# Loading v on all 128 partitions, and keeping attention's packed values and last results in SBUF, in a fused attention and two-MLP kernel

## The chip, the cores and the metric

The kernel runs on one core of a Trainium2 chip. The time is device microseconds of one execution; lower is better. Three runs of the kernel before took 1675.51, 1675.57 and 1678.95 us, with a median of 1675.57 us. Five engines work at once and meet only at semaphores: TensorE (PE, with its weight loads shown as PEld), VectorE (DVE), ScalarE (ACT), GpSimd (POOL) and SyncE (SP), which issues nearly all DMA transfers.

## The reference

Three stages follow each other. First comes an attention that is done twice: 32 learned rows p per head attend to k and v of that head and give 32 packed values; then each row of q attends to these 32 values. There are 8 batches of 8 heads, 576 positions and 64 columns a head.

```python
scale = 1.0 / np.sqrt(q.shape[-1])
def sm_attn(qq, kk, vv):
    s = scale * np.matmul(qq, kk.transpose(0, 1, 3, 2))
    s = s - np.max(s, axis=-1, keepdims=True)
    a = np.exp(s)
    a = a / (np.sum(a, axis=-1, keepdims=True) + 1e-09)
    return np.matmul(a, vv)
p_packed = sm_attn(p, k, v)
out = sm_attn(q, p_packed, p_packed)
```

The result, as 4608 tokens of 512 columns, goes through two MLPs with 2048 hidden columns. The first has a rational function in its middle, the second h * cos(h).

```python
h = x @ w_in
h2 = h * h
h3 = h2 * h
P = a[0] + a[1] * h + a[2] * h2 + a[3] * h3
Q = 1.0 + np.abs(b[0]) * np.abs(h) + np.abs(b[1]) * h2
g = P / (Q + 1e-06)
x = g @ w_out                    # first MLP
h = x @ w_in2; g = h * np.cos(h) # second MLP
out = g @ w_out2
```

All four weight matrices come as 64-bit floats, 8 MB each, and are turned into 32-bit ones on the chip.

## The kernel before, in words

**Attention** works in 16 units u, each of one batch and four heads. For a unit, `load` (lines 435 to 452) brings p, k, q and v into SBUF, three buffers each. `trans` (L468) turns k and q on PE in nine 128x128 transposes each, and `copied` (L474) takes them from PSUM on ACT. `scores` (L497) multiplies p with k, in eight matmuls that use 64 rows and 32 columns of the array. `max1`, `exp1` (L515) and `recip1` are the softmax. `turn_exp` (L533, L535) turns the exponentials, four 128x128 transposes and two narrow matmuls, because the positions have to lie on the partitions for the next product. `pack` (L548) multiplies them with v in 20 matmuls: v lies in SBUF as [128 partitions, 4 heads, 5 pieces, 64], where the fifth piece fills only 64 partitions. `packed`, `turned` and `taken` scale and turn the packed values into the tile `lhpp`. `scores` once more multiplies q with them, and a second softmax (`turn2`, `max2`, `less_max2`, `exp2`, `sum2`, `recip2`, `scaled2`, `turn_back`) gives the tile `a2T`, which `keep_attn` (L606) writes to DRAM. `keep_pack` (L566) writes `lhpp` to the DRAM tensor `ppt`.

Where v is loaded, six transfers make a unit: four of 32 partitions with runs of 256 floats, and two of 32 partitions with runs of 64 floats (L446, L448).

**First MLP.** Its 128 items are 16 half batches c of eight pieces i. The packed values are folded into the first weights: `m_load` (L667) reads `ppt` back into the tile `pt`, and `m_prod` (L692) multiplies it with w_in1. Each batch needs four such products, which `m_hi` (ACT) and `m_lo` (DVE, L705) split into a high and a low part. An item is then a `front` (L737, 12 matmuls for each of two halves), some 14 steps on ACT, DVE and POOL for the rational function, and four `back` (L774) that multiply with w_out1. **Second MLP.** 144 items of the same form, with another function.

**Weights.** `convert` turns one 128-row piece of a weight: `w_load` brings it into one of two `raw` buffers, `w_exp` and `w_low` (ACT, L359 and L362), `w_abs` and `w_join` (DVE, L368 and L378) rebuild 32-bit floats; for w_out there are also `w_hi` (ACT) and `w_lo` (POOL). The first eight pieces of w_in1 and of w_out1 are turned while attention runs, the other eight of each after it. Of the 16 SBUF places of w_out1 (`wo0` to `wo15`), EARLY = 8 exist from the start. The others lie in memory that attention uses, and open when all of attention is done (`open_right`), together with the PSUM pool that `back` adds into.

**Order.** All instructions are listed as steps with a key. A planner (`Plan.order`) picks steps by key among those that could start, and writes the order of each engine; the table WANTED shifts the key of each kind of step. On the chip each engine runs its list strictly in that order, and SP's transfers are issued in list order too.

Of the kernel before, what the change touches and what calls it, by code (L numbers as in the profile page):

```python
# [9 lines left out]
F32 = mybir.dt.float32  # L10
# [17 lines left out]
class Plan:  # L28
# [14 lines left out]
        "a2_hi": 440, "a2_lo": 373, "a2_load": -22, "absolute": -628, "back 0": 104, "back 1": 169,  # L43
        "clipped": 70, "copied k": 251, "copied q": 43, "cosine": 245, "cubic 0": 228,
        "cubic 1": -452, "denom": -187, "done1": -328, "done2": -87, "doubled": 357, "exp1": 189,
        "exp2": 14, "exp_copied 0": -32, "exp_copied 1": 522, "front 0": -261, "front 1": -372,
        "keep_attn": 271, "keep_out": 425, "keep_pack": 48, "less_max2": -596, "lin 0": -168,
        "lin 1": -278, "load k": 275, "load p": -435, "load q": -220, "load v": 93, "lower 0": -109,
        "lower 1": 78, "m_hi": -93, "m_lo": 32, "m_load": -254, "m_prod": -307, "max1": -559,
        "max2": -95, "open_left": -187, "open_right": 541, "over 0": 72, "over 1": 202, "pack": 436,  # L50
        "packed": -313, "ratio": -102, "recip1": 165, "recip2": 77, "reduced 0": 285,
        "reduced 1": -222, "rounded": 209, "rsqrt": 308, "scaled2": 49, "scores 0": -225,
        "scores 1": 191, "slope": -116, "square": -380, "store": 355, "sum2": 21, "taken p": -208,
        "taken pp": 108, "times": -128, "trans k": 275, "trans q": 147, "turn2": 46,
        "turn_back": -404, "turn_exp": 79, "turned p": 64, "turned pp": 562, "upper 0": -141,
# [6 lines left out]
        "x_load": -33, "x_out": -508,  # L62
# [139 lines left out]
def pack_attention_moe_moe_kernel(  # L202
# [42 lines left out]
    EARLY = 8  # L245
# [24 lines left out]
    for pool, home, tags in (  # L270
# [5 lines left out]
        *((f"pt{g}", "cp", (f"pt{g}",)) for g in range(NG)),  # L276
# [8 lines left out]
        ("x0", "xp", ("x0",)),  # L285
# [10 lines left out]
        ("lhpp", "tp", ("lhpp0", "lhpp1")),  # L296
# [6 lines left out]
        ("a2T", "tp", tuple(f"a2T{i}" for i in range(9))),  # L303
# [15 lines left out]
    ppt = dram("ppt", NU, [P, P])  # L319
# [115 lines left out]
    def load(u, nm):  # L435
# [3 lines left out]
        if nm == "p":  # L439
            nc.sync.dma_start(t[:, 0, :], p[b, hs].rearrange("h n d -> (h n) d"))  # L440
        elif nm == "v":


            rows = v[b, hs].rearrange("h (p c) d -> p h c d", c=2 * NT9)
            for j in range(4):
                nc.sync.dma_start(t[32 * j : 32 * (j + 1), :, 0:4, :], rows[:, :, 4 * j : 4 * j + 4, :])  # L446
            for e in range(2):
                nc.sync.dma_start(t[32 * e : 32 * (e + 1), :, 4, :], rows[:, :, 16 + e, :])  # L448
        else:

            src = {"k": k, "q": q}[nm]
            nc.sync.dma_start(t, src[b, hs].rearrange("h (p c) d -> (h p) c d", c=2 * NT9))
# [655 lines left out]
```

## Time and profile before

| what | us |
|---|---|
| median of three runs | 1675.57 |
| the profiled execution | 1677.82 |
| its span | 1675.9 |
| PE busy in the span | 1581.6 (94%) |
| DVE busy | 1289.6 (77%) |
| ACT busy | 1021.1 (61%) |
| POOL busy | 308.3 (18%) |

The profile shows one execution. The span is what the engines' records cover; the execution is 1.9 us longer. A share over the whole span is a mean over attention, the first MLP and the second, which have different limits, so the rows further down split it by stretches of time. The granted clock of PE in a stretch is given as a share of its full 2.4 GHz, so that 0.50 is the lower level of 1.2 GHz. A 32-bit matmul appears in the trace as two passes, each with its weight load; a transpose as one pass.

### The profile page before, as it was taken

To read this page: it belongs to the slowest core of one execution; us is meant where nothing else is said; L and a number is where in the kernel's file an instruction comes from. 1 tells how busy PE (TensorE), PEld (TensorE's weight loads), DVE (VectorE), ACT (ScalarE), POOL (GpSimd) and SP (SyncE) were. 2 spreads that over 40 slices of the span, in tenths; PEclk is the share of its full clock that TensorE was granted. 3 is DMA by queue.
4 is the path that set the end of the run, shared out by engine and by line. 5 is a ranking of instruction groups with operands and counts; after the bars stand their busy time and mean duration, and the time that the engine had idled before them with its cause. 6 is when DMAs were issued, how large, how long until landed. Compare 5 with 4: busy or idle time off the path is not lost.

```text
span 1675.9 us, 26699 instructions
## 1 busy us (share of the span) xinstructions
PE 1581.6 (94%) x10176; PEld 1347.9 (80%) x10176; DVE 1289.6 (77%) x2025; ACT 1021.1 (61%) x1706; POOL 308.3 (18%) x246
## 2 busy tenths in 40 slices
PE   4776579999999999999999999999999999999998
PEld 3444278999999999999998888888888888888887
DVE  2655888999999999999998876666676757576664
ACT  3666788989899899898975543333333334333332
POOL 0223433333343343333321100000000000000000
PEclk7888689999999999999999999999999999999999
DMA  8998431211211121213242210101010101101010
GB/s 253 243 278 243 123 122 36 68 47 64 68 48 63 41 69 60 63 48 135 90 153 84 82 45 7 38 13 38 14 38 8 35 9 26 25 14 38 1 25 26
DMA packets 84383, 120.75 MB, mean 72 GB/s; under 512 B 19232, under 2 KB 61216, under 8 KB 84256
## 3 DMA queue, kind: packets, MB, share of 16 engines
q1 hardware_dynamic: 83872, 118.53, 24.1%
q8 instruction: 80, 1.31, 0.3%
q10 hardware_dynamic: 384, 0.52, 0.1%
q14 instruction: 47, 0.39, 0.1%
HBM read 85.99 MB, written 33.03 MB: 71 GB/s over the span
## 4 chain that ended last, share of the span: by engine, by line
PE 86%; DMA 4%; DVE 4%; ACT 3%; issue 1%; POOL 1%; SPq 1%; POOLq 0%; ACTq 0%
PE acc L774 46%; PE b L753 24%; PE b L737 11%; PE b L692 2%; DMA raw<-in_moe_w_in_dram 1%; PE b L468 1%; PE b L497 1%; DMA v_in<-in_v_dram 1%; DMA raw<-in_moe_w_out_dram 1%; ACT sc L362 0%; DVE T L868 0%; ACT sc L359 0%; DVE U L868 0%; ACT e L515 0%; DMA q_in<-in_q_dram 0%
## 5 line engine op out<-in xcount | busy, mean ns | idle before, releaser
L774 PE MATMUL acc<-gh,wo 128*128 128x288 f32 x2048 | 418.2, 298 | 9.0 <-ACT gh L900 9.0
L774 PE MATMUL acc<-wo,gh 128*128 128x512 f32 x1152 | 359.2, 393 | 0.0
L774 PEld LDWEIGHTS acc<-gh,wo 128*128 128x128 f32 x2048 | 332.0, 190 | 26.9 <-issue 15.9
L774 PE MATMUL acc<-gl,wo 128*128 128x288 f32 x1024 | 304.3, 297 | 1.0 <-DVE gl L903 0.9
L774 PEld LDWEIGHTS acc<-wo,gh 128*128 128x128 f32 x1152 | 216.3, 188 | 49.6
L857 POOL TENSOR_TENSOR U<-U,V 128x576 f32<-128x576 f32 x128 | 182.7, 1437 | 360.8 <-DVE T L872 116.3
L774 PE MATMUL acc<-wo,gl 128*128 128x512 f32 x576 | 226.7, 394 | 0.0
L891 ACT ACTIVATE U<-U 128x512 f32<-128x512 f32 x144 | 90.6, 630 | 203.2 <-DVE U L887 203.1
L903 DVE TENSOR_TENSOR gl<-V,gh 128x512 fp32r<-128x512 f32 x144 | 99.4, 690 | 136.8 <-PE acc L774 135.3
L836 ACT ACTIVATE T<-b 128x512 f32<-128x512 f32 x144 | 85.9, 596 | 187.0 <-PE b L753 186.5
L774 PEld LDWEIGHTS acc<-gl,wo 128*128 128x128 f32 x1024 | 194.0, 189 | 2.1 <-DVE gl L903 2.1
L900 ACT CAST gh<-V 128x512 fp32r<-128x512 f32 x144 | 89.3, 620 | 77.6 <-PE acc L774 72.3
L774 PEld LDWEIGHTS acc<-wo,gl 128*128 128x128 f32 x576 | 108.1, 188 | 24.9
L876 DVE TENSOR_SCALAR T<-T 128x512 f32<-128x512 f32 x144 | 60.9, 424 | 73.9 <-ACT T L836 73.8
L903 DVE TENSOR_TENSOR gl<-T,gh 128x576 fp32r<-128x576 f32 x128 | 111.8, 876 | 7.4 <-PE acc L774 4.7
L894 DVE TENSOR_TENSOR V<-U,b 128x512 f32<-128x512 f32 x144 | 98.3, 683 | 18.0 <-ACT U L891 14.4
L851 ACT ACTIVATE U<-V,par 128x576 f32<-128x576 f32 x128 | 111.0, 874 | 0.8 <-DVE T L872 0.7
L868 DVE SCALAR_TENSOR_TENSOR T<-T,par,V 128x576 f32<-128x576 f32 x128 | 105.4, 842 | 5.0 <-ACT V L864 4.8
L834 ACT ACTIVATE T<-b,par 128x576 f32<-128x576 f32 x128 | 106.2, 831 | 3.6 <-PE b L737 3.0
L883 DVE SCALAR_TENSOR_TENSOR U<-T,U 128x512 f32<-128x512 f32 x144 | 103.6, 720 | 4.0
L848 ACT ACTIVATE V<-b 128x576 f32<-128x576 f32 x128 | 83.2, 651 | 35.1 <-PE b L737 26.0
L845 DVE SCALAR_TENSOR_TENSOR T<-T,par,b 128x576 f32<-128x576 f32 x128 | 101.4, 810 | 3.5 <-ACT V L848 1.4
(182 smaller groups left out, 3059.3 us busy)
## 6 DMA issues: line engine op xcount, KB each, us to landing
raw<-in_moe_w_out_dram SPq DMA_DIRECT2D x32, 512.0 KB, 3.7
q_in<-in_q_dram SPq DMA_DIRECT2D x16, 576.0 KB, 6.0
k_in<-in_k_dram SPq DMA_DIRECT2D x16, 576.0 KB, 7.3
x<-ob SPq DMA_DIRECT2D x16, 576.0 KB, 3.5
raw<-in_moe_w_in_dram SPq DMA_DIRECT2D x32, 256.0 KB, 4.3
v_in<-in_v_dram SPq DMA_DIRECT2D x64, 128.0 KB, 6.2
raw<-in_moe_w_in_dram SPq DMA_DIRECT2D x16, 512.0 KB, 4.6
w<-sc SPq DMA_DIRECT2D x32, 256.0 KB, 2.3
```

The source lines that it names most:

```text
L737: nc.tensor.matmul(TILE["h", j][:, e, 0:HS], lhsT=w[:, o : o + P], rhs=x[:, g, :], start=n == 0, stop=n == 3 * NG - 1,)
L753: nc.tensor.matmul(h, lhsT=w[:, ks], rhs=x, start=n == 0, stop=n == 3 * KC - 1)
L774: nc.tensor.matmul(o, lhsT=w, rhs=x, start=i == 0 and n == 0, stop=i == last and n == len(todo) - 1,)
L834: nc.scalar.activation(T, hidden(j), AF.Identity, scale=par[:, 3:4], bias=par[:, 2:3])
L845: nc.vector.scalar_tensor_tensor(T, T, par[:, 1:2], h, op0=ALU.add, op1=ALU.mult)
L851: nc.scalar.activation(shaped(j, "U"), shaped(j, "V"), AF.Identity, scale=par[:, 5:6], bias=par[:, 4:5])
L857: return nc.gpsimd.tensor_tensor(Q, Q, V, op=ALU.mult)
L868: return nc.vector.scalar_tensor_tensor(t, t, add_, shaped(j, "V"), op0=ALU.add, op1=ALU.mult)
L883: return nc.vector.scalar_tensor_tensor(Y, T, -C2, Y, op0=ALU.mult, op1=ALU.add)
L891: nc.scalar.activation(Y, Y, AF.Sin, bias=PI/2)
L894: nc.vector.tensor_tensor(shaped(j, "V"), shaped(j, "U"), hidden(j), op=ALU.mult)
L903: return nc.vector.tensor_tensor(shaped(j, "gl"), result(j), shaped(j, "gh").bitcast(F32), op=ALU.subtract)
```

## The change

- v is loaded in one transfer a unit, `[128, 2, 9, 64]`: 64 partitions hold two of the heads with nine positions each, the other 64 partitions the other two. Each run in DRAM is then 576 floats.
- The exponentials are written by `exp1` with a stride, so that a position's nine pieces lie apart, and `turn_exp` becomes 18 matmuls of 64x64 in place of four transposes and two matmuls. `pack` becomes 36 matmuls with 64 rows each in place of 20.
- The packed values stay in SBUF: eight `pt` places and the place `x0`, which the second MLP uses later, hold all 16 units. The DRAM tensor `ppt`, `keep_pack` and `m_load` go.
- `kT` and `qT` move into the pool `ld`; the pools of the first MLP's operands open when that pool's users are done, so now after the last `scores`.
- 14 places of w_out1 exist from the start. Attention's last six `a2T` tiles lie in six of them (`wo8` to `wo13`), five other `a2T` places remain of nine, and the last twelve `keep_attn` get other keys.
- WANTED, the units' spacing (UNIT, FROM) and the keys of the weight conversions get new numbers.

```diff
-        "a2_hi": 440, "a2_lo": 373, "a2_load": -22, "absolute": -628, "back 0": 104, "back 1": 169,
+        "a2_hi": 341, "a2_lo": 242, "a2_load": -149, "absolute": -590, "back 0": 176, "back 1": 127,
...
-    EARLY = 8
+    EARLY = 14
+    HELD = 6
...
-        *((f"pt{g}", "cp", (f"pt{g}",)) for g in range(NG)),
+        *((f"pt{u}", "cp", (f"pt{u}",)) for u in range(NU // 2)),
...
-        ("kT", "tp", ("kT0", "kT1")),
-        ("qT", "tp", ("qT0", "qT1")),
+        ("kT", "ld", ("kT0", "kT1")),
+        ("qT", "ld", ("qT0", "qT1")),
...
-        ("a2T", "tp", tuple(f"a2T{i}" for i in range(9))),
+        ("a2T", "tp", tuple(f"a2T{i}" for i in range(HELD - 1))),
...
-            rows = v[b, hs].rearrange("h (p c) d -> p h c d", c=2 * NT9)
-            for j in range(4):
-                nc.sync.dma_start(t[32 * j : 32 * (j + 1), :, 0:4, :], rows[:, :, 4 * j : 4 * j + 4, :])
-            for e in range(2):
-                nc.sync.dma_start(t[32 * e : 32 * (e + 1), :, 4, :], rows[:, :, 16 + e, :])
+            nc.sync.dma_start(t, v[b, hs].rearrange("(n i) (p c) d -> (i p) n c d", i=2, c=NT9))
...
+    def left_of(nm, u):
+        if nm == "lhpp" and u >= NU // 2:
+            return TILE["later", 0][:, (u - NU // 2) * P : (u - NU // 2 + 1) * P]
+        return TILE[nm, u]
...
+    def place_of(h):
+        n = h % 2 * 2 + h // 2
+        return slice(n * NP, (n + 1) * NP)
...
-            TILE["e1", u].rearrange("p (a b) -> p a b", a=2),
-            halves(TILE["s", u, 0]),
+            TILE["e1", u].rearrange("q (p t e) -> q e t p", t=NT9, e=2),
+            halves(TILE["s", u, 0]).rearrange("q e (t p) -> q e t p", t=NT9),
...
-        for c in range(4 if a == 0 else 2):
-            first = c % 2 * HS + (c // 2 * P if a == 0 else 2 * P)
-            if a == 0:
-                nc.tensor.transpose(ps[:, c * P : (c + 1) * P], e1[:, first : first + P], ident)
-            else:
-                nc.tensor.matmul(ps[32 * c : 32 * (c + 1), 0:P], lhsT=e1[:, first : first + 32], rhs=ident, start=True, stop=True)
+        for n in range(1 if a else 8):
+            for i in range(2):
+                r = slice(i * D, (i + 1) * D)
+                nc.tensor.matmul(
+                    ps[r, n * D : (n + 1) * D],
+                    lhsT=e1[r, 8 * a + n : S : NT9],
+                    rhs=ident[r, r],
+                    start=True,
+                    stop=True,
+                )
...
-        for c in range(5):
-            for h in range(G4):
-                r, ks = slice(h * NP, (h + 1) * NP), slice(0, D if c == 4 else P)
+        for c in range(NT9):
+            for h in (0, 1, 2, 3):
+                n, i = divmod(h, 2)
+                r = slice(i * D, (i + 1) * D)
                 nc.tensor.matmul(
-                    TILE["ppp", u][r, 0:D],
-                    lhsT=TILE["e1T", u][ks, c, r],
-                    rhs=TILE["v", u][ks, h, c, :],
+                    TILE["ppp", u][place_of(h), 0:D],
+                    lhsT=TILE["e1T", u][r, c, n * NP : (n + 1) * NP],
+                    rhs=TILE["v", u][r, n, c, :],
                     start=c == 0,
-                    stop=c == 4,
+                    stop=c == NT9 - 1,
                 )
...
-    def keep_pack(u):
-        nc.sync.dma_start(ppt[u], TILE["lhpp", u])
...
-    UNIT, FROM = 18.35, -291.5
+    UNIT, FROM = 20.90875, -269.06
...
+        late = u - (NU - HELD)
+        home = ("a2T", ("a2T", u), [P, S], F32) if late < 0 else (f"wo{NF // 2 + late}", ("a2T", u), [P, 2 * DM], F32)
+        go("DVE", 700, turn_back, tail=70, r=[("r", u)], new=[home])
...
-    def m_load(b, g):
-        nc.sync.dma_start(TILE["PT", b, g], ppt[b * NG + g])
...
-                convert(0, f, which, -1473.7 + 32.65 * (f + n + e * NF // 2))
+                convert(0, f, which, -1282.3 + 22.7975 * (f + n + e * NF // 2))
```

The first loads of q, v and k on SP's list before. The names are the program's tiles and tensors (`v_in` an SBUF buffer of v, `in_v_dram` the input), then the shape and how often the row is issued.

```order
L452 DMA q_in_172<-in_q_dram 128x1152
L452 DMA q_in_174<-in_q_dram 128x1152
L452 DMA q_in_176<-in_q_dram 128x1152
L446 DMA v_in_178<-in_v_dram 32x4x256 x4
L448 DMA v_in_178<-in_v_dram 32x4x64 x2
L446 DMA v_in_185<-in_v_dram 32x4x256 x4
L448 DMA v_in_185<-in_v_dram 32x4x64 x2
L446 DMA v_in_192<-in_v_dram 32x4x256 x4
L448 DMA v_in_192<-in_v_dram 32x4x64 x2
L452 DMA k_in_199<-in_k_dram 128x1152
```

The same place on SP's list now.

```order
L446 DMA q_in_156<-in_q_dram 128x1152
L446 DMA q_in_158<-in_q_dram 128x1152
L446 DMA q_in_160<-in_q_dram 128x1152
L442 DMA v_in_162<-in_v_dram 128x2x576
L442 DMA v_in_164<-in_v_dram 128x2x576
L442 DMA v_in_166<-in_v_dram 128x2x576
L446 DMA k_in_168<-in_k_dram 128x1152
```

Between the third q and the first k stand 18 transfers before and three now.

PE's list before where the attention units run steadily (`one` and `b` are PSUM tiles, `e` the exponentials, `e1T` their turned form).

```order
L548 MATMUL one_1813<-v_in_1379,e1T_1562 32x64 x20
L468 MATMUL b_1836<-ident,q_in_1411 128x128 x5
L533 MATMUL one_1859<-ident,e_1_1738 128x128 x4
L468 MATMUL b_1_1865<-ident,q_in_1571 128x128 x4
L468 MATMUL b_1874<-ident,k_in_1605 128x128 x5
L535 MATMUL one_1884<-ident,e_0_1803 32x128 x2
L468 MATMUL b_0_1888<-ident,k_in_1605 128x128 x4
```

About the same place on PE's list now.

```order
L535 MATMUL one_2078<-ident,e_0_2012 64x64 x16
L535 MATMUL one_2098<-ident,e_0_2012 64x64 x2
L458 MATMUL b_1_2101<-ident,q_in_1667 128x128 x4
L458 MATMUL b_2110<-ident,k_in_1718 128x128 x5
L458 MATMUL b_0_2121<-ident,k_in_1718 128x128 x4
L555 MATMUL one_2134<-v_in_1735,e1T_2079 32x64 x36
```

A unit's turn of the exponentials is now 16 and 2 small matmuls (L535) in place of 4 transposes and 2 matmuls, and its product with v is 36 matmuls (L555) in place of 20.

PE's list before at the end of attention (`lhpp` the packed values as left operand, `pt` the copy read back, `m00h` a split product).

```order
L692 MATMUL b_1_2258<-s_657,pt_724 32x512 x2
L692 MATMUL b_1_2258<-s_1005,pt_724 32x512 x2
L497 MATMUL b_2275<-qT_2125,lhpp_2228 32x288 x8
L737 MATMUL b_0_2306<-a_0_2214,m00h 128x288 x2
L737 MATMUL b_0_2306<-a_0_2214,m00l 128x288
L737 MATMUL b_0_2306<-a_0_2214,m01h 128x288 x2
```

The end of attention on PE's list now.

```order
L555 MATMUL one_2525<-v_in_2185,e1T_2489 32x64 x36
L474 MATMUL one_2579<-ident,pp_2526 128x128
L498 MATMUL b_0_2587<-qT_2447,x_1545 32x288 x8
L700 MATMUL b_1_2613<-s_179,pt_445 32x512 x2
L700 MATMUL b_1_2613<-s_392,pt_445 32x512 x2
```

The products with w_in1 (L692, now L700) stood ahead of the last two `scores` before, and four items' fronts ahead of the very last one; now all of them stand behind the last `scores`.

## Rows read from the trace of the kernel before

**Rows 1.** The page's slices: busy tenths in 40 equal slices of the span.

```profile
PE   4776579999999999999999999999999999999998
...
DMA  8998431211211121213242210101010101101010
```

**Rows 2.** Busy us by stretch, each engine, granted clock, DMA share, GB/s.

```profile
core 0: us, PE busy (x) PEld busy (x) DVE busy (x) ACT busy (x) POOL busy (x), PEclk, DMA share, GB/s
0.00:25.00 25.00, 5.49 (x24) 4.60 (x24) 2.89 (x7) 6.88 (x12) 1.48 (x9) 0.89 0.83 224
25.00:165.00 140.00, 105.30 (x1521) 65.76 (x1521) 79.10 (x176) 86.26 (x175) 38.43 (x44) 0.82 0.93 262
165.00:205.00 40.00, 21.30 (x151) 11.83 (x151) 33.56 (x51) 30.09 (x49) 18.89 (x15) 0.69 0.46 122
205.00:273.00 68.00, 51.92 (x362) 46.83 (x362) 59.29 (x81) 55.20 (x90) 22.86 (x17) 0.88 0.32 100
273.00:868.00 595.00, 594.64 (x4625) 568.97 (x4625) 571.40 (x774) 538.15 (x858) 207.23 (x147) 1.00 0.21 70
868.00:1676.00 808.00, 802.99 (x3496) 649.91 (x3494) 543.41 (x939) 304.54 (x525) 19.42 (x15) 1.00 0.11 31
```

**Rows 3.** One line's instructions: min/median/max ns, first and last start in us.

```profile
L603 DVE STREAM_TRANSPOSE a2T<-r x16: 758/778/779, 50.8 to 203.8; 128x576 f32<-128x576 f32 x16
```

**Rows 4.** The same, of the matmuls with v, and of k's transposes.

```profile
L548 PE MATMUL one<-v_in,e1T x640: 216/219/316, 36.5 to 164.7; 128*32 128x64 f32 x128, 64*32 64x64 f32 x32
...
L468 PE MATMUL b<-ident,k_in x144: 272/273/476, 25.3 to 145.0; 128*128 128x128 f32 x144
```

**Rows 5.** SP's queue in order of time: start us, us, what.

```profile
5.75 1.38 SPq L452 DMA_DIRECT2D q_in<-in_q_dram  x3
7.73 2.64 SPq L446 DMA_DIRECT2D v_in<-in_v_dram  x4
...
20.03 0.90 SPq L448 DMA_DIRECT2D v_in<-in_v_dram  x2
20.98 1.38 SPq L452 DMA_DIRECT2D k_in<-in_k_dram  x3
```

**Rows 6.** The chain from 25 to 60 us: start us, us, what.

```profile
20.98 4.21 DMA k_in<-in_k_dram
...
25.32 2.17 PE b L468 x9
...
42.26 0.72 PE b L497 x16
42.98 0.59 PE one L533 x4
43.56 0.34 PE one L535 x4
...
44.68 0.83 PE one L548 x40
```

**Rows 7.** Two short stretches: first v alone, then k and q.

```profile
14.00:20.00 6.00, 2.62 (x13) 2.06 (x12) 0.00 (x0) 1.86 (x3) 0.00 (x0) 0.96 0.80 176
...
24.00:28.00 4.00, 2.15 (x9) 1.78 (x9) 0.00 (x0) 1.18 (x2) 0.00 (x0) 0.50 1.02 374
```

**Rows 8.** DMA issues from 0 to 165 us: count, KB each, median us to landing.

```profile
q_in<-in_q_dram SPq DMA_DIRECT2D x16, 576.0 KB, 6.0
...
v_in<-in_v_dram SPq DMA_DIRECT2D x64, 128.0 KB, 6.2
raw<-in_moe_w_in_dram SPq DMA_DIRECT2D x16, 256.0 KB, 5.8
...
v_in<-in_v_dram SPq DMA_DIRECT2D x32, 32.0 KB, 5.2
ppt<-lhpp SPq DMA_DIRECT2D x13, 64.0 KB, 5.4
```

**Rows 9.** The chain of waits from 0 to 300 us.

```profile
60.77 1.14 PE b L468 x9
```

More of the change, by code (lines that the diff above doesn't have):

```diff
@@ L49 @@
[L49 to L54, printed above, removed]
@@ L55 @@
-        "turn_back": -404, "turn_exp": 79, "turned p": 64, "turned pp": 562, "upper 0": -141,
[6 rows of a table removed]
-        "x_load": -33, "x_out": -508,
+        "a2_hi": 341, "a2_lo": 242, "a2_load": -149, "absolute": -590, "back 0": 176, "back 1": 127,
+        "clipped": 201, "copied k": 627, "copied q": 46, "cosine": 154, "cubic 0": 337,
+        "cubic 1": -426, "denom": -162, "done1": -89, "done2": -339, "doubled": -169, "exp1": 212,
+        "exp2": 52, "exp_copied 0": 409, "exp_copied 1": 706, "front 0": 4, "front 1": 102,
@@ new lines @@
+        "keep_attn": 83, "keep_out": 836, "less_max2": -794, "lin 0": 202, "lin 1": -215,
+        "load k": 327, "load p": -781, "load q": -306, "load v": 260, "lower 0": -346,
+        "lower 1": 169, "m_hi": 472, "m_lo": -218, "m_prod": -699, "max1": -539, "max2": -358,
+        "open_left": 198, "open_right": 781, "over 0": 194, "over 1": 151, "pack": 835,
+        "packed": -16, "ratio": -313, "recip1": 643, "recip2": 21, "reduced 0": 193,
+        "reduced 1": -270, "rounded": 157, "rsqrt": 503, "scaled2": 275, "scores 0": -306,
@@ L63 @@
+        "scores 1": 315, "slope": -298, "square": -583, "store": 386, "sum2": 182, "taken p": -159,
+        "taken pp": 522, "times": 324, "trans k": 505, "trans q": 267, "turn2": 18,
+        "turn_back": -611, "turn_exp": 199, "turned p": 128, "turned pp": 629, "upper 0": -132,
[6 rows of a table added]
+        "x_load": -695, "x_out": -552,
     }
@@ L458, in piece @@
         return flat2(TILE[nm + "ps", u, j])[:, 0 : (t1 - t0) * P]
-    def pair_of(nm, t):
-        return 2 * (t % 4) + t // 4 if nm == "k" and t < 8 else t
     def trans(u, nm, j):
@@ L495, in scores @@
             for h in range(G4):
-                r = slice(h * NP, (h + 1) * NP)
+                r, to = slice(h * NP, (h + 1) * NP), place_of(h)
                 nc.tensor.matmul(
-                    TILE["s", u, k][r, e, 0:HS],
-                    lhsT=TILE[lhs, u][rows, r],
+                    TILE["s", u, k][r if k else to, e, 0:HS],
+                    lhsT=left_of(lhs, u)[rows, to if k else r],
                     rhs=of_head(TILE[rhs, u][rows], h),
@@ L661, in attention @@
         go("POOL", 1110, scaled2, r=[("mx", u)], w=[("r", u)])
-        go("DVE", 700, turn_back, tail=70, r=[("r", u)], new=[("a2T", ("a2T", u), [P, S], F32)])
-        go("SP", 60, keep_attn, r=[("a2T", u)], w=[("a2 out", u)], kb=290, key=FROM + u * UNIT + (24 if u < NU - 9 else 6))
-    def m_load(b, g):
-        nc.sync.dma_start(TILE["PT", b, g], ppt[b * NG + g])
+        late = u - (NU - HELD)
+        home = ("a2T", ("a2T", u), [P, S], F32) if late < 0 else (f"wo{NF // 2 + late}", ("a2T", u), [P, 2 * DM], F32)
+        go("DVE", 700, turn_back, tail=70, r=[("r", u)], new=[home])
+        go("SP", 60, keep_attn, r=[("a2T", u)], w=[("a2 out", u)], kb=290, key=FROM + u * UNIT + (24 if u < NU - 2 * HELD else 95 - 5 * u))
     def a2_load(c):
@@ L693, in m_prod @@
                     TILE["mps", b, a, g][r, e, :],
[L694 removed]
+                    lhsT=left_of("lhpp", b * NG + g)[rows, place_of(h)],
                     rhs=TILE["win1", k2][rows, o * DM : (o + 1) * DM],
@@ L957, in operands1 @@
         if hf == 0:
-            for g in range(NG):
-                add("SP", 60, first - 50, m_load, b, g, r=[("kept", b * NG + g)], new=[(f"pt{g}", ("PT", b, g), [P, P], F32)], kb=64)
             for a in range(2):
@@ L963, in operands1 @@
                     wins = [("win1", (a * H + g * G4) // 2 + i) for i in range(2)]
-                    add("PE", 1024, key, m_prod, b, a, g, tail=100, r=[("PT", b, g), *wins], new=[("b2", ("mps", b, a, g), *ps2), *((f"m{a}{g}{e}", ("M", b, a, g, e), [P, 2 * CH], F32R) for e in "hl")], after=opened_at("m00h"))
+                    add("PE", 1024, key, m_prod, b, a, g, tail=100, r=[("lhpp", b * NG + g), *([("later", 0)] if b * NG >= NU // 2 else []), *wins], new=[("b2", ("mps", b, a, g), *ps2), *((f"m{a}{g}{e}", ("M", b, a, g, e), [P, 2 * CH], F32R) for e in "hl")], after=opened_at("m00h"))
                     add("ACT", 905, key, m_hi, b, a, g, tail=100, r=[("mps", b, a, g)], w=[("M", b, a, g, "h")])
```

50 lines of the change are left out of this document (23 added, 27 removed), and 12 rows, old and new, of the table WANTED.

## The prediction

> **What bounds the kernel now.** I read the slices of the page first, then busy time by stretch. In the slices PE is at 9 of tenths from the seventh slice to the last, and DMA only in the first four [rows 1]. So the span is split where PE becomes continuous. By stretch, PE is busy 594.6 of 595 us from 273 to 868 and 803.0 of 808 us from there to the end [rows 2]. After 273 us PE alone sets the time: its work there fills 1403 us, and the change neither removes nor adds any. DVE is close behind until 868 (571 of 595 us), though it does not hold PE up. What can be won or lost is the moment at which PE becomes continuous, now 273 us.
>
> Ahead of it lie four stages. **A**, 0 to 25 us: transfers alone, with PE nearly idle. The chain waits there for the first k, and k's transposes begin at 25.3 us [rows 4, 6]. **B**, 25 to 165 us: attention's units run, and DMA is busy 0.93 of the time at 262 GB/s, more than any engine (PE 105, ACT 86, DVE 79 of 140 us) [rows 2]. The sixteenth product with v starts its last matmul at 164.7 us [rows 4]. **C**, 165 to 205 us: attention's last units end (the last turned tile starts at 203.8 us [rows 3]) while conversions and first fronts run, DVE busy 33.6 of 40 us. **D**, 205 to 273 us: DVE 59.3 and ACT 55.2 of 68 us [rows 2], rational functions and the other conversions. So the kernel is bound by transfers, then by DVE with ACT, then by PE.
>
> **The change part by part.**
>
> *v's transfers in stage A.* On SP the first v transfer is issued at 7.73 us and the first k at 20.98, 13.25 us later, for three units of six transfers [rows 5]. Three q's or k's are issued in 1.38 us [rows 5]; three v's of the same form would take about that, so the first k would be issued at about 9 us. Then bytes decide. Through the first k they are about 5.3 MB: 1.05 of w_in1 (four transfers of 256 KB), 0.1 of p, and 0.59 (576 KB) for each of three q's, three v's and one k [rows 8]. At the 374 GB/s of k and q [rows 7] that is 14 us; with 2.3 us until the first packets and 2 us to land, k would be there at about 18.5 us; with v at a rate between the two rows, at 20 to 21. I take **-5 us**, bounds 0 (no better rate) and -8.
>
> *v's transfers in stage B.* While v alone is moved, the rate is 176 GB/s, and with k and q 374 [rows 7]. Thirteen units remain, 7.67 MB: 43.6 us at 176, 20.5 us at 374. The trace has no 128-partition transfer of runs of 2304 bytes. The bounds are no gain (the short runs were not the reason) and 23 us; the nearest row is that of q and k, one transfer over 128 partitions, so I take 23 us less DMA time.
>
> By the Trainium skill, "DMA: Bandwidth & Descriptors", Specifications, a transfer runs at line rate from 512 B a run, which speaks against this: four fifths of v already move in runs of 1024 B. By that rule only the fifth with 256 B runs would gain, some 4 us. The trace does not agree, since the stretch with v alone shows 176 GB/s.
>
> *The packed values' transfers.* Thirteen of the 16 stores, 64 KB each [rows 8], lie in stage B, 0.85 MB: 2.3 us at 374 and 4.8 at 176 GB/s; I take 3.5. Nothing waits for the reads back. Together DMA in stage B falls from 130 us (0.93 of 140) to 130 - 23 - 3.5 = **103.5 us**.
>
> *PE in stage B.* A unit's product with v takes 0.83 us for 40 passes, 0.0208 us each; the turn of the exponentials 0.59 + 0.34 us [rows 6]. That is 1.76 us. Now there are 72 and 36 passes. From below: all at 0.0208 us, 2.24 us, or 0.48 us more a unit, 7.7 us for 16. From above: the narrow turn has four passes of 128 columns in 0.34 us, 0.085 us each, so 0.0425 for 64 columns if nothing overlaps; 108 such passes make 4.6 us, 2.8 us more a unit, 45 for 16. I take the lower one, since `scores`, which likewise uses half the rows and a quarter of the columns a matmul, does 16 passes of 288 columns in 0.72 us [rows 6], 0.045 us each; without overlap the narrow turn's rate would give 0.19. PE's busy time in B becomes 105.3 + 8 = **113 us** at the granted clock of 0.82. At the full clock, k's nine transposes take 1.14 us where they take 2.17 at the lower level [rows 6, 9], and 105.3 us would be about 105.3 x 0.82 = 86, so 94 with the addition.
>
> *ACT and DVE in stage B* keep their work: 86 and 79 us. The strided write of `exp1` is not shown by any row; I cost it at nothing because ACT has 54 us of idle time there. It would have to cost over 1.5 us a unit to make ACT the longest.
>
> *Stage B as a whole.* Before, the longest resource needed 130 us and the stage took 140, a ratio of 1.077. Now the longest is PE with 113; 113 x 1.077 = 122, **-18 us**. The bounds: DMA at 103.5 with PE at its full clock gives 111 (-29); PE at the upper price is a rival below.
>
> *Places and order.* k's and q's turned tiles now close their pool later, so the products with w_in1 stand behind the last `scores`. These wait for turning and scores of the last unit, some 2 us (0.72 for `scores` [rows 6] and its ahead steps), unhidden if DVE has nothing else. I take **+2 us**; bounds 0 and one unit's turn, scores and product, about 4. The last a2T tiles in places of w_out1 and the five other places cost nothing as long as SP's stores of them go out before the conversions need the places; those conversions come in stage D, tens of us later. If that cover fails, a conversion waits for one store. Stages C and D keep the same steps on DVE (93 us) and ACT (85 us) and are only moved forward. PE from 273 us on keeps its work.
>
> *Sum.* -5 - 18 + 2 = -21 us against the profiled execution of 1677.8 us: 1656.8. The median of the runs shown is 2.2 us below that execution, so I predict 1654.6, say **1655 us**.
>
> **The rivals.**
>
> *1. Transfers are not what paces stage B.* k's transposes run from 25.3 to 145.0 us [rows 4], which is 8 us a unit, while DMA needs 130/16 = 8.1. A unit passes from engine to engine, and the engines' lists are strictly ordered. If that chain paces the units, faster v transfers change only stage A. For it: PE, ACT and DVE are all busy over half of the stage. Against it: DMA at 0.93. It gives -5 + 2 = -3 us, 1672.6.
>
> *2. The small matmuls do not overlap, at full clock.* Both halves of the rows now write one PSUM tile, whereas `scores` writes two different halves of its tile, so the row of `scores` may not carry over. Then PE needs 86 + 45 = 131 us, the stage 141: +1 - 5 + 2 = -2 us, 1673.6.
>
> The Trainium skill, "TensorEngine Tiling (Array Packing)", Gotcha 1, says that different row tiles cannot access the same PSUM bank simultaneously. By that rule halves of the rows would take turns, which is this rival; no row of before shows two row halves in one tile.
>
> *3. The same, at the clock that the stage has now: slower.* With PE granted 0.82, 105 + 45 = 150 us, times 1.077 is 162: +22 - 5 + 2 = +19 us, 1694.6. The place is PE's list in stage B, the price 2.8 us a unit. It decides from the point where stage B exceeds 143 us, PE at 133, that is 1.7 us more a unit or 0.032 us a pass. For it: the clock in that stage fell to 0.5 more than once, as where the first k's are turned [rows 7]. Against it: PE shows a clock of 1.00 wherever it is continuous [rows 2], and a PE that paces the stage would be nearly that.
>
> *4. More than forecast.* Stage B follows DMA, 111 us, and k arrives 8 us earlier: -29 - 8 = -37, 1638.6.
>
> **How the numbers follow.** Forecast 0.62, rival 1 0.12, rival 2 0.06, rival 3 0.10, rival 4 0.10. Two measurements of this kernel differ by up to about 0.2% (3.4 us), so "same" is 1672.2 to 1678.9. Faster: forecast, rival 4 and half of rival 1, 0.78. Same: the other half and rival 2, 0.12. Slower: rival 3, 0.10. The range goes from rival 4 to rival 2, **1638 to 1674**; it leaves out rival 3 and whatever lies below rival 4.
>
> **What would show it.** In the new profile: the first transposes of k at 18 to 21 us instead of 25.3; v's transfers gone from the slow rate, and DMA's busy share in attention's stretch below 0.93; the last product with v at 140 to 147 us instead of 164.7; PE continuous from about 252 instead of 273 us, and 1400 us of continuous PE behind it. A unit's product with v at about 1.5 us would confirm the pass price; 3 us would be rivals 2 or 3, told apart by the granted clock of the stage. If the last product with v comes at about 160 us while DMA's share falls, it is rival 1. The forecast is wrong altogether if PE shows new waits after it has become continuous, since all of the argument rests on that part being only moved.

## The result: slower, and the profile after

Timed in turn with the kernel before, five executions each, the changed kernel takes 1686.69 us against 1678.05 (medians): a ratio of 1.0055, interval 1.0039 to 1.007. The forecast of 1655 us and its whole range lie below that. The profiled execution took 1685.71 us, its span 1683.8, which is 7.9 us more than the span of before.

First the stretches of [rows 2] again, of the kernel after (columns as there):

```profile
0.00:25.00 25.00, 10.32 (x55) 8.05 (x55) 3.64 (x8) 8.11 (x15) 1.41 (x9) 0.89 0.92 292
25.00:165.00 140.00, 117.53 (x2257) 88.79 (x2260) 78.65 (x173) 87.75 (x166) 38.95 (x44) 0.85 0.76 242
165.00:205.00 40.00, 26.57 (x357) 18.43 (x349) 30.23 (x49) 29.52 (x49) 18.10 (x14) 0.82 0.43 122
205.00:273.00 68.00, 50.99 (x337) 45.31 (x337) 57.00 (x82) 56.72 (x93) 22.75 (x17) 0.85 0.27 82
273.00:868.00 595.00, 593.99 (x4614) 566.37 (x4615) 570.16 (x772) 538.16 (x855) 206.58 (x147) 1.00 0.21 70
868.00:1676.00 808.00, 807.30 (x3521) 655.90 (x3520) 556.93 (x945) 308.83 (x529) 20.80 (x17) 1.00 0.11 30
```

DMA's share from 25 to 165 us fell from 0.93 to 0.76, and PE's time rose from 105.3 to 117.5 us. From 273 us on PE is as continuous as before. So nothing was lost there, and yet everything there comes later. Each line's first and last start shows by how much (the numbers behind the count are min/median/max ns; the answers to [rows 3, 4]):

```profile
L516 ACT ACTIVATE e<-b,sm x16: 1318/1342/1372, 25.7 to 173.7; 128x576 f32<-128x576 f32 x16
L535 PEld LDWEIGHTS one<-ident,e x576: 191/214/218, 27.1 to 177.1; 64*64 64x64 f32 x192
L555 PE MATMUL one<-v_in,e1T x1152: 216/216/313, 32.3 to 179.8; 64*32 64x64 f32 x192
L607 DVE STREAM_TRANSPOSE wo<-r x6: 720/772/778, 144.2 to 195.8; 128x576 f32<-128x576 f32 x6
L745 PE MATMUL b<-a,m00h x256: 288/295/609, 187.2 to 836.0; 128*128 128x288 f32 x128
L761 PEld LDWEIGHTS b<-a,s x288: 186/188/192, 862.2 to 1530.7; 128*128 128x128 f32 x144
```

and the same lines of before that were not shown ahead:

```profile
L515 ACT ACTIVATE e<-b,sm x16: 736/741/761, 31.4 to 147.9; 128x576 f32<-128x576 f32 x16
L753 PEld LDWEIGHTS b<-a,s x288: 186/188/192, 853.7 to 1517.5; 128*128 128x128 f32 x144
```

The first exponential starts 5.7 us earlier, the last one 25.8 later. The last product with v moves from 164.7 us to 179.8. The second layer's first front (L761, L753 before) comes at 862.2 instead of 853.7 us, 8.5 later: that is the loss. It arises ahead of 273 us, and not at the end of attention: the last turned result (195.8 us, 203.8 before) is even earlier, while the first front (L745) starts at 187.2 us, 9.9 later than before (177.3).

What changed there is seen in the chain of waits, one unit after another (start us, us, what; compare [rows 6]):

```profile
9.98 9.53 DMA k_in<-in_k_dram
...
19.65 2.17 PE b L458 x9
...
97.39 2.39 PE one L535 x36
99.78 0.65 PE b L498 x16
100.43 0.69 PE b L458 x5
101.12 2.31 PE one L535 x36
103.44 0.59 PE b L458 x4
104.02 2.14 PE one L555 x144
...
109.48 0.66 DVE sm L510
...
110.22 1.35 ACT e L516 x2
```

The turn of the exponentials (L535) takes 2.3 to 2.4 us a unit, where it took 0.59 + 0.34 at the same granted clock of 1.00. The two products with v (L555, 144 passes) take 2.14 us, 1.07 each, also at 1.00. Of the chain from 25 to 165 us the turn has the largest part, 24.1%, and the exponential 9.6%:

```profile
by line: PE one L535 24.1%; PE b L458 13.0%; ACT e L516 9.6%; issue 9.0%; PE b L498 7.4%; PE one L555 6.4%; DVE r L579 3.4%; DVE sm L510 3.0%; ACT kT L464 2.7%; POOL r L588 2.5%; ACT r L592 2.1%; DVE mx L584 2.0%; ACT qT L464 1.7%; DVE sc L
```

And what SP's queue waited for, 25 to 165 us (total us, times, longest), first before, then after:

```profile
SPq L452 <- DMA raw<-in_moe_w_out_dram: 6.2, 3, 2.4
SPq L452 <- DMA k_in<-in_k_dram: 5.6, 4, 2.3
```

```profile
SPq L446 <- PE b L458: 31.2, 14, 5.5
SPq L350 <- DVE sc L377: 31.0, 6, 10.1
SPq L442 <- PE one L555: 17.6, 8, 6.9
```

Before, the longest waits of the queue were for earlier transfers. After, a load of k, q or v waits until PE has used up what stands in its place (31.2 and 17.6 us), and a piece of w_out (L350) until VectorE has used up the buffer of an earlier one (31.0 us), with the loads behind it in the list standing too: the loads follow the engines. What the waits for w_out cost was not tested by itself; without strides (e3 and e16 below) they are 26.6 and 26.5 us.

### The profile page after: what moved, and what is told of

It reads as the page before. It is cut to its first block, busy times and chain, and to the rows that moved or that the text cites. A ratio compares the mean times of both kernels' runs of the same rounds, so it can differ in the third digit from the quotient of the medians.

```text
span 1683.8 us, 28427 instructions
## 1 busy us (share of the span) xinstructions
PE 1609.7 (96%) x11136; PEld 1385.0 (82%) x11136; DVE 1298.0 (77%) x2025; ACT 1030.3 (61%) x1706; POOL 308.6 (18%) x246
## 4 chain that ended last, share of the span: by engine, by line
PE 86%; ACT 6%; DVE 3%; issue 3%; DMA 1%; POOL 1%; SPq 0%; ACTq 0%; DVEq 0%; POOLq 0%
PE acc L782 45%; PE b L761 24%; PE b L745 11%; PE one L535 2%; PE b L700 2%; PE b L458 1%; ACT e L516 1%; DMA raw<-in_moe_w_in_dram 1%; PE b L498 1%; PE one L555 1%; DMA k_in<-in_k_dram 1%; ACT sc L358 1%; ACT U L859 1%; ACT V L856 0%; DVE T L876 0%
## 5 line engine op out<-in xcount | busy, mean ns | idle before, releaser
L876 DVE SCALAR_TENSOR_TENSOR U<-U,V 128x576 f32<-128x576 f32 x128 | 101.7, 806 | 10.1 <-ACT V L872 9.8
L911 DVE TENSOR_TENSOR gl<-T,gh 128x576 fp32r<-128x576 f32 x128 | 104.8, 822 | 3.3 <-PE acc L782 1.8
L851 DVE TENSOR_TENSOR T<-T,b 128x576 f32<-128x576 f32 x128 | 94.1, 745 | 11.1 <-ACT T L842 10.8
```

What stands on the lines that cost most here:

```text
L851: nc.vector.tensor_tensor(T, T, h, op=ALU.mult)
L876: return nc.vector.scalar_tensor_tensor(t, t, add_, shaped(j, "V"), op0=ALU.add, op1=ALU.mult)
L911: return nc.vector.tensor_tensor(shaped(j, "gl"), result(j), shaped(j, "gh").bitcast(F32), op=ALU.subtract)
```

## The experiments

Theory S: reading and writing `e1` with a stride is what costs. The exponential writes 32-bit values 72 bytes apart, and the turn reads its weights 36 bytes apart; both are steps of each unit's chain. Rivals: the number of small passes costs (rivals 2 and 3 of the prediction); the order of the engines' lists does, since the keys and the pools were changed too; or the faster transfers were worth little to begin with (rival 1). Each run was timed in five rounds beside the kernel before. Ratios are to before; us are medians.

**Strides taken away, lists kept as they are.** e1 changes the write, e2 the read, e3 both. The three put other positions together than the reference, with the same work in number and size.

```diff
 # e1                      TILE["e1", u].rearrange(
-    "q (p t e) -> q e t p"
+    "q (e t p) -> q e t p"
 # e2
-    lhsT=e1[r, 8 * a + n : S : NT9],
+    lhsT=e1[r, (8 * a + n) * D : (8 * a + n + 1) * D],
```

> The changed kernel with one edit: the exponentials are written in the order of the scores, without a stride between neighbours, while the turn reads as before the edit (so the positions that the turn puts together are other ones than the reference's; the work is the same in number and size, and so is every engine's list). Theory 1 (the strided layout of the exponentials makes each attention unit's chain longer, by 0.6 us in the exponential and by 1.5 us in the turn): the exponential falls from 1.34 to 0.74 us and the whole by 4 to 9 us, to about 1680. Theory 2 (the new order and pools cost the time: products with w_in1 behind the last scores, the new key table): the exponential falls too, but the whole by at most 2 us, staying at 1684 to 1687.

> The changed kernel with one edit: the turn of the exponentials reads 64 neighbouring columns a matmul in place of every ninth column (other positions are put together than in the reference; same number of matmuls, same lists). Theory 1: the 32 passes of the larger turn fall from 2.14 us to 0.9 to 1.4 us, and the whole by 8 to 16 us, to about 1674. Theory 2: the passes fall, the whole stays within 3 us of 1686. If the passes stay at 2.1 us, the number of the weight loads and not their stride sets the turn's price.

> Both edits together: exponentials written without a stride and turned from neighbouring columns (other positions are put together than in the reference; same lists). Theory 1: the sum of both, 14 to 22 us less than the changed kernel, about 1668, so below the kernel before, with the last product with v at 160 us or earlier instead of 180. Theory 2: within 4 us of the changed kernel, 1683 to 1687.

e1 took 1678.83 us, ratio 1.0009 [0.9999, 1.002]; e2 1674.88, 0.9985 [0.9976, 0.9994]; e3 1672.07, 0.9966 [0.9955, 0.9977]. Against 1686.69 the write is worth 7.9 us alone, the read 11.8 alone, both 14.6: less than their sum, and no run shows why. These are the gains that theory S expected (theory 1 in the texts above); only the last product with v, at 164.8 us in e3, comes later than the 160 expected. In e3 both durations fall, at the same count and shape:

```profile
L516 ACT ACTIVATE e<-b,sm x16: 722/740/761, 26.3 to 160.2; 128x576 f32<-128x576 f32 x16
...
L535 PEld LDWEIGHTS one<-ident,e x576: 128/135/229, 27.4 to 162.1; 64*64 64x64 f32 x192
```

Its chain has the turn at 96.9 us in half the time; the windows over one turn of e3, and over one of after, show the granted clock (the third number from the end) at 1.00 in both:

```profile
96.90 1.19 PE one L535 x36
```

```profile
96.90:98.10 1.20, 1.20 (x37) 1.13 (x38) 0.98 (x3) 1.16 (x3) 0.67 (x2) 1.00 1.06 375
```

```profile
111.60:114.00 2.40, 2.38 (x37) 2.31 (x38) 0.61 (x3) 1.63 (x4) 1.94 (x2) 1.00 1.03 397
```

So at equal clock 36 passes take 1.19 to 1.26 us (0.034 a pass) with neighbouring values and 2.4 us (0.067) with strided ones. With 0.60 us of the exponential the strides cost 2.39 - 1.26 + 0.60 = 1.73 us a unit at this clock; that makes an estimate of 28 us in 16 units, of which 14.6 reach the end.

**The same, with the stride put on the other side.** e12 iterates so that `e1` is written side by side and PSUM is read with the stride instead; the turn stays strided.

```diff
-    TILE["e1", u].rearrange("q (p t e) -> q e t p", ...),
-    halves(TILE["s", u, 0]).rearrange("q e (t p) -> q e t p", ...),
+    TILE["e1", u].rearrange("q (p t e) -> q p t e", ...),
+    halves(TILE["s", u, 0]).rearrange("q e (t p) -> q p t e", ...),
```

> The changed kernel, same lists and same layout of the exponentials in SBUF, but the exponential goes through them position by position, so that it writes neighbours one after the other and reads PSUM with the strides instead. If the price of 0.6 us lies in the strided writes alone: 0.74 us an exponential and the time of the run with unstrided exponentials, 1676 to 1681. If strided reads of PSUM cost as much: 1.2 us or more and 1684 to 1688.

1679.4 us, 1.001 [1.0002, 1.0019], which is e1's result, with the exponential at its old duration:

```profile
L516 ACT ACTIVATE e<-b,sm x16: 723/741/770, 26.9 to 167.6; 128x576 f32<-128x576 f32 x16
```

It is the strided write to SBUF that costs ScalarE; the strided read of PSUM costs it nothing here.

**The faster transfers alone.** e9 is the kernel before with its lists unchanged; v comes as two transfers over all partitions, and its values then lie at other positions than the reference's.

```diff
-    rows = v[b, hs].rearrange("h (p c) d -> p h c d", ...)   # and six transfers
+    flat = t.rearrange("p h c d -> p (h c d)")
+    rows = v[b, hs].rearrange("h (p c) d -> (h p) (c d)", c=2 * NT9)
+    nc.sync.dma_start(flat[:, 0 : 2 * NT9 * D], rows)
+    nc.sync.dma_start(flat[:, 2 * NT9 * D :], rows[:, 0 : 2 * D])
```

> The kernel before with every engine's list unchanged; only v's six transfers a unit become two over 128 partitions, of 576 KB and 64 KB (v's values then lie at other positions than the reference's; nothing else changes). It shows what faster transfers of v are worth by themselves. If transfers pace attention, as my sum had it (-5 us ahead of the first k, -18 us after it): 15 to 22 us less than before, 1655 to 1662. Rival 1 (the chain of a unit through the ordered lists paces it): only the gain ahead of the first k and little more, 3 to 8 us less, 1669 to 1674.

1674.07 us, 0.9982 [0.9972, 0.9991]: about 3.2 us below before, near the -3 of rival 1 and far from the -23 of stages A and B. k's first transposes begin at 21.1 us, 4.2 earlier than before, so the gain is no larger than what is won ahead of the first k. The rate was there (first line, v and then k), and DMA's share from 25 to 165 us fell from 0.93 to 0.80:

```profile
12.00:20.00 8.00, 4.67 (x22) 4.27 (x21) 0.00 (x0) 2.56 (x4) 0.00 (x0) 1.00 1.03 410
```

```profile
25.00:165.00 140.00, 103.11 (x1526) 64.63 (x1518) 82.47 (x183) 88.84 (x180) 40.92 (x45) 0.86 0.80 260
```

Its queue now waits longest not for transfers but for results that it is to store, which stand in the list ahead of loads:

```profile
SPq L604 <- DVE a2T L601: 20.2, 8, 5.4
SPq L564 <- ACT lhpp L487: 16.8, 7, 4.6
```

**v over 96 partitions.** e13 is the kernel before, its lists unchanged, with six pieces of 96 positions: no strided access to `e1`, six turns of 96 columns, and 24 matmuls for the product (48 passes, where after has 72). e14 also issues the packed values' stores from ScalarE's queue, and e15 the results' stores too.

```diff
+    nc.sync.dma_start(t[0:96], v[b, hs].rearrange("h (p c) d -> p h c d", c=6))
 # exp1
+    TILE["e1", u].rearrange("q (e y b) -> q e y b", e=2, b=3),
+    halves(TILE["s", u, 0]).rearrange("q e (b y) -> q e y b", b=3),
 # turn_exp, c in 4 and 2; pack, c in 6
+    nc.tensor.transpose(ps[0:96, c * P : (c + 1) * P], e1[:, n * 96 : (n + 1) * 96], ident)
 # e14: keep_pack, e15: keep_attn too
-    nc.sync.dma_start(...)
+    nc.scalar.dma_start(...)
```

> A complete version with the lists of the kernel before: v in one transfer a unit over 96 partitions (runs of 384 floats), exponentials read from PSUM with strides and written one after the other, six transposes of 96 neighbouring columns, and a product with v of 24 matmuls. No strided writes, no strided weight loads, four matmuls more than before. Expected as the run with fast transfers and unchanged lists: 1670 to 1676, 1 to 7 us less than the kernel before. If the 96-column turn or copies cost on the chain: 1677 to 1682.

> The same, with the 16 stores of packed values issued from ACT's queue instead of SP's, at the place in ACT's list that the planner gave them. If SP's ordered list withholds the transfers' gain: SP's waits for these stores (17 us in stage B) go and the time falls by 2 to 6 us more, to 1666 to 1673. If the units' chain through the engines sets the pace alone: within 2 us of the run before it.

> The same, with the stores of attention's results on ACT's queue too. If SP's list withholds the gain: SP's waits in stage B fall below 15 us and the time by 2 to 8 us more than with the packed values alone, unless ACT then waits for DVE's results ahead of its own work, which would show as waits on ACT and a time above the run before it. If the units' chain sets the pace: no gain from either.

e13: 1678.16 us, 1.0 [0.9991, 1.0009]. e14: 1676.12, 0.9995 [0.9985, 1.0004]. e15: 1687.1, 1.0057 [1.0043, 1.007]. e13 misses its 1670 to 1676 and gains nothing. Its turn and copies need not be the reason, as the expectation's other branch has it: v over 96 partitions is slow as well. From 12 to 20 us, where e9 moves 410 GB/s, e13 moves 239, and k's first transposes begin at 25.1 us, hardly before those of before (25.3):

```profile
12.00:20.00 8.00, 3.94 (x22) 3.49 (x20) 0.00 (x0) 2.46 (x4) 0.00 (x0) 0.89 1.10 239
```

The 4.0 us by which the first k comes later than in e9 are about the 4.1 between the two times. e14 is 2.0 us faster than e13, but their intervals overlap. In e14 SP's wait for `lhpp` is gone, and the profile puts its waits down to the moved store instead:

```profile
SPq L443 <- DMA ppt<-lhpp: 13.9, 2, 7.2
```

In e15 ScalarE itself stands still for results that it is to store, with the next units' work behind it:

```profile
ACT kT L465 <- DVE a2T L592: 6.6, 2, 3.8
ACT lhpp L480 <- DVE a2T L592: 2.5, 1, 2.5
```

Moving the waiting instruction to another queue moved the wait; with the results' stores on ScalarE's queue too it cost 11 us against e14. Since v is slow in all three, they don't show whether SP's waits for stores are what withholds the gain in e9; that stays open.

**What the order of the lists is worth.** e10 is before with the new table of keys; e11 is after with the old table; e7 before with the new pools and held results, old keys; e4 after with the v part undone; e5 before with the v part alone, and e6 the same without strides. In these the planner put out other lists than either kernel's.

```diff
 # e10: before, e11: after, the other way round
-    "a2_hi": 440, "a2_lo": 373, ...
+    "a2_hi": 341, "a2_lo": 242, ...
 # e7: before
-    EARLY = 8
+    EARLY = 14
+    HELD = 6
-        ("kT", "tp", ("kT0", "kT1")),
+        ("kT", "ld", ("kT0", "kT1")),
 # e4: after with six transfers of v, e5: before with
+    nc.sync.dma_start(t, v[b, hs].rearrange("(n i) (p c) d -> (i p) n c d", i=2, c=NT9))
 # e6: e5 with the two edits of e3
```

> The kernel before with only the numbers of the change: the new key table, unit spacing and conversion keys; all operations, transfers and pools stay. Only the order of the lists changes. If the order of the lists is worth as much as the parts that the change is about: 8 to 20 us slower than before, 1685 to 1697. If order hardly matters: within 3 us of 1677.

> The changed kernel with the old key table, unit spacing and conversion keys. If a table fits only the program that it was made for: slower than the changed kernel, 1690 to 1702. If the new table itself is a bad one: faster than the changed kernel, 1670 to 1682.

> The kernel before with only the other part of the change, and with the old keys: packed values kept in SBUF, the last six results in places of w_out1, five other places, k's and q's turned tiles in the pool of the loads. With the new keys and the old v the same kernel took 1690.6 us. Theory 2a (the key table made that loss): with the old keys at most the time of before, 1670 to 1679. Theory 2b (the pools made it: products with w_in1 behind the last scores): 1684 or more.

> The changed kernel with v's part undone: v in six transfers a unit, exponentials, turn and product with v as in the kernel before; packed values and last results stay in SBUF, new keys and pools stay. Theory 1: what v's layout cost on the chain goes and its faster transfers go with it, so about the time of the kernel before or a little less, 1672 to 1680. Theory 2: the new order and pools alone hold the loss, so 1684 or more.

> The kernel before with only v's part of the change: one transfer of v a unit, strided exponentials, the turn in 18 matmuls and the product with v in 36; old keys, old pools, packed values through DRAM. Theory 1 (strides cost about 15 us, faster transfers give back only part): 3 to 10 us slower than before, 1681 to 1688. Theory 2 (the loss comes from keys and pools): at most the time of before, 1665 to 1678.

> The same with the exponentials written without a stride and turned from neighbouring columns (other positions are put together than in the reference; same lists as the run before it). It shows what v's transfers are worth without the strides' price. If transfers paced attention in the kernel before, as my sum had it: 12 to 20 us less than before, 1658 to 1666. If engines and their lists paced it as well (rival 1): about 3 to 8 us less, 1670 to 1675. Theory 1: 10 to 16 us less than the run before it.

e10: 1686.81 us, 1.0058 [1.0038, 1.0078]. e11: 1705.43, 1.0174 [1.0157, 1.019]. e7: 1696.27, 1.0106 [1.009, 1.0123]. e4: 1690.56, 1.0082 [1.0069, 1.0096]. e5: 1695.26, 1.0104 [1.009, 1.0118]. e6: 1684.69, 1.0043 [1.003, 1.0056]. All six are slower than before. As expected were e10 (1685 to 1697) and the difference between e5 and e6; e5, e6 and e11 came out above their ranges. e4 and e7 came out where the new order and pools alone hold the loss (1684 or more), but in lists that neither kernel has. From e5 to e6 the strides go and 10.6 us come back, in quite other lists, the same in both: theory S once more. The rest shows that a table of keys fits its own program: the same operations in an order made for another program cost 9 us (e10) and 19 us (e11). What keys, pools and held results each contribute can't be read from these runs.

**Another way without strides.** e8 is after with v laid out like k and q, the exponentials turned by VectorE in tiles of 32 x 32, and 72 matmuls of 32 rows (new lists).

```diff
-    for n in range(1 if a else 8): ...            # PE's turn, and two copies
+    nc.vector.transpose(TILE["e1T", u], TILE["e1", u])
```

> A version meant to keep v's single transfer without strides: the changed kernel with v loaded like k and q (32 partitions a head, 18 positions each), exponentials written in score order, turned by one VectorE transpose of 32x32 blocks in place of 18 matmuls and two copies, and a product with v of 72 small matmuls. Theory 1: like the run with both strides away or better, 1664 to 1674; the turn is 0.78 us on DVE in place of 2.4 us on PE and 0.8 us of copies, the product with v 2 to 3 us in place of 1.1. Theory 2: 1682 or more.

1705.09 us, 1.016 [1.0145, 1.0175], 31 us above the range expected. Its lists are new too, so this doesn't say what VectorE's turn costs by itself.

**Both findings together.** e16 has the lists of the changed kernel and v over 96 partitions as in e13; a2T has four places instead of five, for room.

```diff
-    ("a2T", "tp", tuple(f"a2T{i}" for i in range(HELD - 1))),
+    ("a2T", "tp", tuple(f"a2T{i}" for i in range(HELD - 2))),
```

> The changed kernel with its lists of instructions as they are, v over 96 partitions of six pieces of 192 positions, so that the exponentials are written side by side (PSUM is read with a stride instead), the turn takes 96 neighbours a pass in six passes instead of nine strided ones, and the product with v has 24 passes instead of 72; a2T has four places instead of five, to make room. The output is complete. Theory of the strides: their 14.6 us come back, as in e3 (1672.1): 1669 to 1675, below both kernels, exponentials about 0.74 us each instead of 1.34, weight loads of the turn about 0.13 us instead of 0.21. Rival, the layout of 96 costs as it did in e13 against e9 (1678.2 against 1674.1, both in the lists of before): 1675 to 1679. Rival, a2T's place matters, since its writer waits for the products of w_out: above 1680.

1667.24 us, 0.9933 [0.992, 0.9945]: 11.0 us below before and 19.5 below the changed kernel, the fastest of all and below its own range. (A piece has 96 positions, not the 192 of the expectation.) Attention's stretch from 25 us to its last product with v lasts 134.5 us; in e3 it lasts 139.8, though there DMA is far less busy:

```profile
25.00:159.50 134.50, 99.75 (x1646) 64.44 (x1646) 91.74 (x193) 87.90 (x183) 44.37 (x49) 0.88 0.92 262
```

```profile
25.00:164.80 139.80, 109.89 (x2492) 79.20 (x2490) 89.00 (x193) 88.57 (x182) 44.53 (x49) 0.90 0.77 249
```

Neither e3 nor e16 has strides. e16 also has fewer passes: 6 a unit for the turn where e3 has 36, and 48 for the product where e3 has 72 (the expectation's 24 and 72 should have been 48 and 72). And it has another layout, so the 4.8 us between them have no single cause shown. It isn't the transfers of v: over 96 partitions they are slow here too, 254 GB/s from 12 to 20 us, and k's first transposes begin at 22.8 us.

```profile
12.00:20.00 8.00, 3.01 (x18) 2.66 (x17) 0.00 (x0) 2.46 (x4) 0.00 (x0) 0.83 1.10 254
```

e13 and e16 take v, turn it and multiply with it in the same way, and differ in all the rest of the change: keys and lists, pools, packed values and last results kept in SBUF. e13 gains nothing, e16 11 us. So what e16 gains comes from that rest as a whole, in the lists made for it; which part of it is not shown. With v's fast transfers the same step, from e9 to e3, is worth 2.4 us (-3.2 to -5.6), but e3 has more passes than e9 as well.

## Why the prediction was wrong, step by step

The forecast was -21 us, and +8.6 was measured. Half of the gap is the strides, priced at nothing and worth 14.6 us. The other half is in the rest of the sum: without strides, in the same lists (e3), the change gives -5.6 and not -21.

*k's first arrival (-5).* Right: k's transposes begin at 19.65 us instead of 25.3, inside 18 to 21.

*The transfers' own time in stage B.* Right as a size, wrong as a term. The forecast had 103.5 us of DMA; the share of 0.76 in 140 us makes 106, that of 0.71 up to the last product with v (154.8 us) 110. The rate from 12 to 20 us is 399 GB/s (v, then k):

```profile
12.00:20.00 8.00, 4.04 (x20) 3.67 (x19) 0.00 (x0) 2.56 (x4) 0.00 (x0) 0.96 1.03 399
```

*"I take the lower one", all passes at 0.0208 us.* Half right. The product with v was expected at about 1.5 us and took 1.07 at a granted clock of 1.00, 0.015 us a pass. That is less than the 0.0208 of the full-height passes of before, so the two row halves that write one PSUM tile didn't take turns in a way that costs time, and rivals 2 and 3 fall as mechanisms. (The Trainium skill, "TensorEngine Tiling (Array Packing)", Gotcha 1, says that different row tiles can't access the same PSUM bank simultaneously; the time of these passes doesn't show it.) The turn was the failure: 36 passes at 0.067 us instead of 0.0208, 2.4 us instead of 0.75, and beyond even the upper bound of 0.0425. It was priced by `scores` and by the old narrow turn, whose rows both read neighbouring values; no row had a strided read of weights, and the stride was not priced on that side at all.

*"I cost it at nothing because ACT has 54 us of idle time there."* This is the first step that failed outright. The strided write costs 0.60 us a unit. The idle time of a stretch would cover it only if no one waited for the exponential; but the turn, the copies and the product of the unit do, and L516 is on the chain. e1 gives 7.9 us for this step alone. The Trainium skill, "SBUF — State Buffer", Specifications (TRN2), says that at least two hits in a line of 16 bytes are needed for full bandwidth; both strides here (72 and 36 bytes) have one, and the rows agree: an exponential takes 1342 ns against 740, a weight load of the turn 214 against 135.

*"Now the longest is PE with 113; 113 x 1.077 = 122, -18 us."* The second step that failed. Up to its last product the stretch has PE at 128.0 us and lasts 154.8, a ratio of 1.21 and not 1.077:

```profile
25.00:179.80 154.80, 128.00 (x2489) 97.00 (x2488) 88.24 (x193) 96.83 (x183) 44.74 (x49) 0.85 0.71 226
```

Even with the right PE time the rule would have given 138, better than before. No engine is busy throughout (PE 0.83 of that stretch), and DMA's share is 0.71. A unit passes through PE, ACT and DVE in an order written into their lists, and the transfers are issued when those lists have freed a place. That a lower DMA load doesn't shorten the stretch in proportion is shown: e9 gains 3.2 us in the lists of before at a DMA share of 0.80, and e16 at 0.92 is faster than e3 at 0.77. That the chain through the lists is what sets the pace instead is argued from the waits; no run isolates it. Rival 1, at 0.12, had this mechanism: its -3 us with the strides' 14.6 make +11.6, where +8.6 was measured (6.5 to 11.7 by the interval). That its -3 is so near the -3.2 of e9 is partly luck: it is -5 for the first k and +2 for places and order, and e9 has nothing of the second.

*Rival 3* named a place (PE's list in stage B) and a deciding price (1.7 us more a unit) that came true: turn and product together take 3.47 us instead of 1.76. Its reason, row halves that take turns, did not.

*Places and order (+2, places at nothing).* As one term it is mis-sized, and its parts are not settled. In the changed kernel the last `scores` start at 182.5 us and the first products with w_in1 at 183.0, so they do stand behind them, and PE stands idle for 6.3 us of the 11.6 ahead of that. SP waits 12.0 us for results held in w_out1's places up to 300 us, 5.0 of them before 165 ("SPq L610 <- DVE wo L607"); the profile puts no wait of a conversion down to such a store. All of this part with its lists is worth -11 us between e13 and e16, and -2.4 between e9 and e3, which has more passes; neither is +2. The runs that were to separate it were planned anew, and the order alone moved them by more than the term.

*Only moved from 273 us on.* Right: PE is busy 593.99 of 595 us up to 868 (594.64 before), and 807.30 of 808 after it.

## What to carry to other kernels

Before a stretch is scaled by its busiest resource, look whether its queue waits for transfers or for the results of engines, and whether a step lies on the chain of one unit: an engine's idle share covers nothing that the next engine waits for. Price an access with a stride as an operation of its own, on both sides of the tile; if a layout saves transfers by making the engines hop, weigh it against one that doesn't. Here 96 partitions instead of 128 gave up most of the transfers' gain (254 instead of 399 GB/s) and still made the fastest kernel. A table of keys that orders the work is part of the program: try an edit with the instruction lists held still first, or the order's own 9 to 19 us hide what the edit does.

## What was not expected of the hardware

- A 128 x 576 exponential written 72 bytes apart takes 1.34 us instead of 0.74; written side by side and read from PSUM with a stride, it stays at 0.74.
- A 64 x 64 turn whose weights are read 36 bytes apart takes 0.067 us a pass, with neighbours 0.034 at a granted clock of 1.00, and about 0.06 (2.18 us for 36) at 0.51. Strided, the clock hardly mattered: 0.068 us a pass at 0.50 (2.19 us for 32, from 27.1 us of after), 0.066 at 1.00 (2.39 for 36).
- 72 passes of 64 rows into one PSUM tile, both row halves, run at 0.015 us a pass, where full-height passes took 0.0208 (both at a granted clock of 1.00).
- v over 96 partitions with runs of 384 floats moves only somewhat faster than in six transfers of 32 partitions: 221 GB/s from 14 to 20 us in e13, where before has 176 in [rows 7], while v over 128 partitions, and k behind it, move 399 to 410 from 12 to 20 us.
